# Shift filter of k in 32-row TensorE tiles, with compact diagonals, 1,024-wide gating, 512 KB exchanges and fourteen dummy matmul groups

## The chip, the cores and the metric

One core of one Trainium2 chip runs the whole kernel. The metric is the device time of one execution in microseconds (us). The kernel before takes 215.59 us in the median of its first three runs (215.18 to 217.14), and between 214.3 and 215.4 in the median of the later groups of runs. In the profile PE is TensorE (matmul), PEld its weight loads, DVE is VectorE, ACT is ScalarE, POOL is GpSimd and SP is SyncE, which issues the DMA transfers.

## The reference

Two blocks with residuals over x of 2,048 positions by 512 features, bf16. Cut to what matters:

```python
def _A_ref(q, k, v, shift_k, ssm_k, ssm_D):           # q is the layernorm of x
    k_pad = jnp.pad(k, ((0, 0), (ks - 1, 0), (0, 0)))  # ks = 4 taps
    for t in range(ks):                                # the shift filter of k
        k_shift = k_shift + k_pad[:, t:t + S, :] * shift_k[:, ks - 1 - t][None, None, :]
    kv = k_shift * v                                   # the gating
    y = irfft(rfft(kv, 2 * S) * rfft(ssm_k, 2 * S))[:S]   # a long convolution, feature by feature
    return q * (y + kv * ssm_D)
h  = x + _A_ref(layernorm(x), ...)
h2 = h + _B_ref(layernorm(h), w1, w2, w3, w4)          # two gelu MLPs, 512-512-512 and 512-1792-512
```

## The kernel before

The convolution is a Fourier transform in two steps on TensorE. Step 1 (`S1`) transforms within blocks; ScalarE or VectorE evacuates each result from PSUM (`E1`); an exchange by DMA (`X`) moves the parts to the partitions where step 2 (`S2`) needs them; its results are evacuated (`E2`), multiplied (`P`) and transformed back (`I2`, `EV`, an exchange `XI`, `I1`). `F0` is the convolution kernel, `A0` and `A1` are kv's first and second half. After it come the MLPs (`W`, `X2`, `M`, `O`). The time order of all tasks on all engines is fixed by a list in the source, `ORDER`, and semaphores keep it; so each engine runs its own tasks strictly in turn.

The shift filter (`K`) runs on TensorE as multiplication with diagonal matrices that hold the taps: k^T is the stationary operand (128 features by 128 positions) and four 128x128 diagonals of taps are the moving one. VectorE then multiplies with v (`KV`).

```python
    def fill(e, sl):                                       # a dummy group: keeps TensorE busy in waits
        for i in range(6):
            nc.tensor.matmul(ps[:, sl[0], 0:P], lhsT=ident[:], rhs=ident[:], start=True, stop=True)
    ...
        for g in range(2):
            for kl in range(4):
                def f(e, s, g=g, kl=kl):                   # one exchange: 256 KB, two of four blocks
                    nc.sync.dma_start(z2[sig][g:P:2, kl, :, :], z1[sig][kl:P:4, 2 * g:2 * g + 2, :, :])
    ...
    def shift(g, c):                                       # 16 groups: g = half and its half, c = 128 features
        s, b4 = divmod(g, 2)
        def f(e, sl):
            o = ps[:, sl[0], :]                            # one PSUM bank, 512 columns
            for i, d in enumerate((0, 1, 2, 3, -1, -2, -3)):   # 7 matmuls
                j0, j1 = max(0, -d), min(3, 3 - d)
                ...
                nc.tensor.matmul(o[:, (d + j0) * P:(d + j1 + 1) * P], lhsT=kT[s][c][:, bb, x:x + P],
                                 rhs=diag[:, c, j0:j1 + 1, :].rearrange("p j x -> p (j x)"), start=(i == 0), stop=(i == 6))
        return f
    def gating(g, c): ...                                  # 16 multiplies of 512
```

In an `ORDER` word the letter is the engine. `M` is a special one: it merges two evacuations of 1,024 columns into one of 2,048 on ScalarE.

Of the kernel before, what the change touches and what calls it, by code (L numbers as in the profile page):

```python
# [9 lines left out]
P = 128  # L10
# [3 lines left out]
DC = D // P  # L14
# [17 lines left out]
031V 002S 021P7 022P 027P6 059P01 005S 061P23 060A 041V 003S 063P45 065P67 033V 037V 099P10 091P01 000S 042G 001S 032V 043V 049V 062A 066A 008S 036G  # L32
040V 046V 055P23 057P67 064A 105P5 007S 035G 039A 047V 056A 010S 058A 103P4 106V 006S 034G 038A 048A 050V 004S 067P23 068A 069P67 070A 097P5 009S 018S
100V 044V 092V 098V 051A 045A 104V 101P1 019S 102V 093P0 094V 346V 095P5 096V 119P23 120A 115P01 116V 015S 117P67 118A 012S 121P45 122A 107P23 011S
108V 109P01 111P67 112V 113P45 110A 017S 344V 348V 114A 183P30 184V 013S 072S 076S 082P0167 084A 187P5 029P4 071S 075S 079P2367 020S 350V 128S 185P4
347V 188V 083A 127S 123S 053G 081A 124S 080A 351V 186V 125S 131P0167 133V 132A 343G 134P2345 136A 028P1 026P7 129S 137P0145 135A 016S 138A 054G 143V0
144V1 145P67230 147V2 139A 130S 146V3 148P 153V0 152V1 156V2 077S 149A 191P11 150A 073S 085P4567 087A 030P0 074S 192V 155V3 154P01231 157P 025P7 086A
158M 159A 349V 345V 024P6 126S 140P4567 141A 078S 151S 162V0 088P0123 089A 014S 161V1 160S 164V2 142V 352G 353G 354G 163P45670 165V3 170V0 166P 189P1
090A 171V1 174V2 168A 173V3 193P0 190V 172P23671 175P 177V 197P1 198V 167A 169S 052A 176A 178S 203P45 204A 205P67 206A 355G0 194V 195P3 196V 199P01
201P45 202A 358G1 340S 207P23 237S 200V 211P67 212A 217S 213P01 179P54 359V 364G1 180P76 356V 214A 361G0 235S 023P1 365V 208A 238S 236S 209P23 360A  # L40
357A 181P54 210A 362V 370V1 371V 379G 380G 367V0 366A 247P01 248A 249P23 376G1 363V 239P67 250A 182P10 240A 381V 251P23 377V 339S 382V0 252A 241P67
242A 392G 393G 219S 385V1 368V 373G0 383P00 386P4 387A 243P23 245P67 369A 372V 405G 406G 244A 253P45 254A 384V 390P0 391A 394V 395V0 396P31 398V1 374V
375A 399P2 246A 216S 397V 388P1 389A 400V 215S 223P2345 403P0 225A 378V 418G 407V 408V0 222S 221S 409P70 404A 411V1 412P6 220S 218S 224V 260S 262S
256S 413V 410V 275V0 401P1 402A 257S 276V1 278V2 229P2345 230A 419G 420G 424V0 259S 231A 414P7 415A 416P6 421V1 417A 266P0123 268V 267V 422P50 425P4
426A 261S 435P7 423A 436V 437A 431P6 432V 269P2345 433A 429P1 271V 430A 279V3 427P7 428A 232P4501 234A 342S 270V 233A 455G 439P7 440V 441A 443P6 444V
445A 456G 457G 461G0 255S 263P0123 264V 451P7 452V 265V 458G1 459P60 226P4501 460A 462P6 447P7 484G 485G 486V 228A 463A 258S 487V0 277P01230 280P
488A1 227A 281V0 282V1 285V2 341S 284V3 464P60 465A 474P5 490S 475A 283P 448V 290V0 286P 288A 272P4567 449A 291V1 273V 287A 453A 640G 641G 472P3 294V2
473A 476P2 292P01451 293V3 295P 274V 489S 477A 491S1 492P30 493A 496P7 296V0 497A 502P6 503A 642G 644A0 297V1 299V2 298P 300V3 306V0 301P 303A 302A
498P7 305V1 500P6 501A 504P5 505A 499A 446V 494P4 289S 307P01230 308V2 309V3 311V0 304S 310P 646S 495A 509P7 312V1 313P 438V 315V2 643V0 645S 314V3
316P 317M 318A 506P6 321V0 510V0 320V1 323V2 511S 322P01231 513S 324V3 325P 326V0 470P7 471A 327V1 329V2 468P5 469A 466P4 512S 330V3 518V 328P 331P  # L50
519V 467A 478P7 481P5 514S 516V 517V 332M 333A 521V 515S 522V 319S 523V 647S1 520V 524V 525G 442V 507V0 526V 530V0 334S 335P64 531V 532A 527G1 336P32
337P10 648P40 528V 529A 649A 536G0 537V 533G1 551V 552G 650P6 652P2 534V 542A0 543V 539G1 538A 653A 535A 651A 548A0 553V 554V0 660P4 658P3 659A 654P0
655A 555P60 557V1 540V 558P2 559A 541V 564G 565G 656P1 544V 576G 566V 556A 568V0 570S 567V1 338P03 545A1 546V 549V 569S 657A 577G 578V 661A 579V0 581S
580V1 582S 560P6 561A 482V1 483S 547A 550A 588G 589G 562P2 590G 662P4 571S0 563A 600P6 604P5 605V 606A 591G0 665P3 583S1 601V 574P6 575A 572P5 573A
592G1 584P2 585A 602V 586P6 587A 668V 450V 593S 669G 670V 671A0 616P6 617V 672G1 594S 595S0 596P5 597A 598P6 599A 620P2 434V 479V1 624P5 618V 636P7
621V 623V 622A 696V 628P6 697G 637V 674S 673S 632P2 675S0 676P70 686P1 480S 682P0 698V 700A0 699V1 701S 625V 626A 612P5 633V 702S 629V 678P6 608P2
677A 703S1 680P7 609V 630A 454V 724V 725G 683A 679A 638A 688P6 689A 726G 727A0 663V1 687A 664S 681A 611V 728V1 730S 613V 634V 780G 729S 684P2 685A
603V 704P00 712P6 705A 710P4 666V1 713A 614A 708P5 706P7 707A 714P3 610V 752V 711A 508S 731S0 709A 690P2 691V0 692S 716P7 732P60 744P2 781G 782G 753G
667S 693P5 754G 755A0 619V 756V1 758S 742P4 717A 745A 639V 733A 715A 734P7 735A 721P6 740P7 718P3 757S 722V0 738P6 736P2 759S1 784G1 760P10 772P0 607V
694V1 766P5 695S 737A 739A 770P6 635V 783G0 785S 723S 741A 743A 746P7 773A 762P4 786S 787S0 788P20 800P0 789A 801A 719V1 627V 767A 792P3 720S 793A  # L60
790P2 791A 798P5 799A 796P0 797A 794P3 795A 771A 747V0 748S 764P5 768P0 769A 805P7 806V0 749P0 807S 765A 761A 763A 631V 750V1 615V 751S 774P7 775V0
776S 802P6 803V1 804S 777P7 778V0 779S
# [40 lines left out]
def body(ctx, tc, fx, kt, q, v, sd, w1, w2, w3, w4, out):  # L103
# [69 lines left out]
    diag = r_dg[:].rearrange("p (c j x) -> p c j x", c=DC, j=4)  # L173
# [7 lines left out]
    hbt = ct("hbt", 2, D)  # L181
    junk = {"A": ct("junka", D, dt=mybir.dt.uint8), "V": ct("junkv", D, dt=mybir.dt.uint8)}
# [57 lines left out]
    make_identity(nc, ident[:])  # L240
    ui, us = ti[0][:, 0:512], ti[1]
# [10 lines left out]
    for o, terms in enumerate((((4, 16), (2, 8), (0, 4), (1, 2), (5, 1)), ((6, 64), (7, 1)), ((3, -1024), (7, 3072)), ((3, 3072),),  # L252
                               ((5, 4), (6, 8), (0, 128), (1, 256), (2, 512), (3, 1024), (4, 2048)), ((5, 64), (0, 16), (1, 32), (7, 1)),
                               ((3, -3072), (7, 3072)), ((4, 2), (2, 1)))):
        for b, w in terms:
            pool.memset(wf[:, o, b:b + 1], float(w))
# [50 lines left out]
    for i in range(8):  # L307
        add(("fill", i), {PEc: 0.36}, fill, ["wend"], take=[("ps", 1)], drop=[(("fill", i), 0)])
# [5 lines left out]
    def dg(c):  # L314
        def f(e, sl):
            for j in range(4):
                sc = sskf[:, 4 * c + j:4 * c + j + 1]
                if e == GP:
                    pool.tensor_scalar(out=diag[:, c, j, :], in0=ident[:], scalar1=sc, scalar2=0.0, op0=MUL, op1=ADD)
                elif e == A:  # L320
                    act.activation(diag[:, c, j, :], ident[:], ACT.Copy, scale=sc)
                else:
                    vec.tensor_scalar(out=diag[:, c, j, :], in0=ident[:], scalar1=sc, scalar2=None, op0=MUL)  # L323
        return f
    for c in range(DC):
        add(("dg", c), {V: 0.8, A: 1.19, GP: 1.45}, dg(c), [("skf", c)], port="VG")
# [82 lines left out]
    def forward1(sig, src, sdeps, zdeps, xdeps=(), sdrop=None):  # L409
# [7 lines left out]
        for g in range(2):  # L417
            for kl in range(4):
                def f(e, s, g=g, kl=kl):
                    nc.sync.dma_start(z2[sig][g:P:2, kl, :, :], z1[sig][kl:P:4, 2 * g:2 * g + 2, :, :])  # L420
                add(("X", sig, g, kl), {SP: 0.62}, f, [("E1", sig, b, hp) for b in (2 * g, 2 * g + 1) for hp in range(2)] + list(xdeps), size=256)
# [10 lines left out]
    def forward2(sig):  # L432
        for kl in range(4):
            n = ("S2", sig, kl)
            add(n, {PEc: 0.46}, step2(sig, kl), [("X", sig, g, kl) for g in range(2)] + ["ft"], take=[("ps", -2)], mode=2)
# [11 lines left out]
    def shift(g, c):  # L447
        s, b4 = divmod(g, 2)

        def f(e, sl):  # L450
            o = ps[:, sl[0], :]
            for i, d in enumerate((0, 1, 2, 3, -1, -2, -3)):
                j0, j1 = max(0, -d), min(3, 3 - d)
                bb, x = 4 * b4 + d, 1
                if bb < 0:
                    bb, x = bb + NB, 0
                nc.tensor.matmul(o[:, (d + j0) * P:(d + j1 + 1) * P], lhsT=kT[s][c][:, bb, x:x + P],  # L457
                                 rhs=diag[:, c, j0:j1 + 1, :].rearrange("p j x -> p (j x)"), start=(i == 0), stop=(i == 6))
        return f
# [396 lines left out]
```

## Time and profile before

| stage (before), us | what runs | what limits it |
|---|---|---|
| 4.5 to 17.4 | loads, transform of the convolution kernel, first half's filter | ScalarE, VectorE, DMA |
| 17.4 to 47.7 | first half's transforms and products, second half's filter | ScalarE |
| 47.7 to 80.6 | inverse, second half's transform, first MLP | ScalarE and TensorE |
| 80.6 to 208.6 | rest of the second half, MLPs | TensorE alone |

The lines of the profile behind this table are in the prediction below. One more from the page, its part on the DMA queues (packets, MB, share of 16 engines):

```profile
q8 instruction: 19, 0.31, 0.6%
```

### The profile page before, as it was taken

How to read it: one execution, taken by the hardware profiler on the slowest of the kernel's cores; microseconds unless marked ns; L12 is line 12 of the kernel's file. 1: busy time of each engine (PE TensorE's matmuls, PEld its weight loads, DVE VectorE, ACT ScalarE, POOL GpSimd, SP SyncE). 2: the span in 40 equal slices, each digit the busy share in tenths (PEclk: the TensorE clock that was granted, in tenths of full speed). 3: DMA queues.
4: the chain of work that ended last, by engine and by line, in shares of the span. 5: the costliest groups of instructions: out<-in, count | busy, mean ns of one | idle time of the engine just before them, and what ended most of it. 6: DMA issues, size and time to landing. Idle time of an engine off the chain costs nothing.

```text
span 212.1 us, 5986 instructions
## 1 busy us (share of the span) xinstructions
PE 198.5 (94%) x2418; PEld 120.5 (57%) x2436; DVE 142.6 (67%) x324; ACT 131.4 (62%) x211; POOL 60.1 (28%) x159
## 2 busy tenths in 40 slices
PE   7899888899899988999999999989999999999993
PEld 5454434543375536874554874756786657686441
DVE  7899999877999989968797883468484043100521
ACT  4998899989999777791360992445484303067000
POOL 7431004915980442300005776301161200000000
PEclk9999999999999999999999999999999999999999
DMA  6999896279939972613493027355235505100101
GB/s 183 301 400 354 311 332 216 104 219 331 400 149 324 354 312 56 151 47 104 144 233 99 3 53 152 79 109 107 49 102 82 118 0 125 51 25 3 47 28 49
DMA packets 31773, 33.44 MB, mean 158 GB/s; under 512 B 22529, under 2 KB 24578, under 8 KB 31490
## 3 DMA queue, kind: packets, MB, share of 16 engines
q1 hardware_dynamic: 31746, 33.06, 50.8%
q8 instruction: 19, 0.31, 0.6%
q14 instruction: 8, 0.07, 0.1%
HBM read 13.13 MB, written 4.72 MB: 84 GB/s over the span
## 4 chain that ended last, share of the span: by engine, by line
PE 64%; DMA 4%; DVE 4%; POOL 2%; ACT 2%; issue 2%; SPq 1%; DVEq 0%; POOLq 0%
PE ps L781 23%; PE ps L793 23%; PE ps L730 5%; PE ps L501 5%; DMA r_y<-r_x 4%; PE ps L701 3%; PE ps L520 2%; POOL z_t L619 1%; DVE r_v L622 1%; PE ps L457 1%; ACT r_h L705 1%; SPq L420 1%; PE ps L404 1%; ACT r_x L266 1%; DVE hbt L656 1%
## 5 line engine op out<-in xcount | busy, mean ns | idle before, releaser
L781 PE MATMUL ps<-r_dg,r_k 128*128 128x256 bf16 x448 | 51.4, 273 | 0.6 <-ACT r_vs L266 0.5
L781 PEld LDWEIGHTS <-r_k 128*128 128x128 bf16 x448 | 43.4, 98 | 8.9 <-issue 2.1
L795 DVE TENSOR_TENSOR r_kv<-ps,r_a 128x512 bf16<-128x512 f32 x5 | 3.5, 692 | 29.7 <-PE ps L793 29.7
L785 ACT ACTIVATE r_kv<-ps 128x512 bf16<-128x512 f32 x21 | 11.8, 601 | 17.2 <-PE ps L781 17.2
L793 PE MATMUL ps<-w4s,r_kv 128*128 128x512 bf16 x81 | 18.8, 379 | 0.2
L266 ACT CAST r_x<-ps 128x1024 bf16<-128x1024 f32 x16 | 15.4, 1026 | 2.3 <-PE ps L404 2.3
L730 PE MATMUL ps<-r_v,r_h 128*128 128x512 bf16 x59 | 15.0, 379 | 1.0 <-ACT r_h L705 0.7
L501 PE MATMUL ps<-r_p,ttab 32*32 32x512 bf16 x768 | 15.1, 379 | 0.8 <-DVE r_p L489 0.4
L457 PE MATMUL ps<-r_dg,r_k 128*128 128x256 bf16 (+3 forms) x109 | 15.3, 286 | 0.5 <-DVE r_dg L323 0.2
L701 PE MATMUL ps<-hnT,r_v 128*128 128x256 bf16 x128 | 15.6, 273 | 0.1
L793 PE MATMUL ps<-w4s,r_f 128*128 128x512 bf16 x62 | 15.0, 379 | 0.1
L266 ACT CAST r_f<-ps 128x1024 bf16<-128x1024 f32 x15 | 14.7, 1033 | 0.5 <-PE ps L428 0.4
L701 PEld LDWEIGHTS <-r_v 128*128 128x128 bf16 x128 | 12.1, 98 | 4.1 <-issue 2.3
L457 PEld LDWEIGHTS <-r_k 128*128 128x128 bf16 x112 | 9.2, 98 | 8.4 <-issue 4.2
L785 ACT ACTIVATE r_f<-ps 128x512 bf16<-128x512 f32 x16 | 9.0, 603 | 7.3 <-PE ps L781 7.2
L793 PEld LDWEIGHTS <-r_kv 128*128 128x128 bf16 x84 | 8.1, 98 | 9.5 <-issue 0.2
L705 ACT ACTIVATE r_h<-ps 128x512 bf16<-128x512 f32 x16 | 9.7, 641 | 4.9 <-PE ps L701 4.9
L501 PEld LDWEIGHTS <-ttab 32*32 32x32 bf16 x768 | 8.3, 88 | 7.0 <-issue 4.9
L607 ACT ACTIVATE junka<-r_q 128x512 uint8<-128x512 bf16 x12 | 7.6, 633 | 7.3 <-DVE r_q L733 7.0
L489 DVE TENSOR_TENSOR r_p<-r_a,r_y 128x1024 bf16<-128x1024 bf16 x16 | 10.1, 685 | 2.9 <-PE ps L501 2.8
L266 ACT CAST r_y<-ps 128x1024 bf16<-128x1024 f32 x12 | 11.4, 1021 | 1.2 <-PE ps L404 1.2
L404 PEld LDWEIGHTS <-f 128*32 128x32 bf16 x256 | 6.1, 95 | 10.3 <-issue 5.7
(179 smaller groups left out, 362.6 us busy)
## 6 DMA issues: line engine op xcount, KB each, us to landing
r_x<-r_vs SPq DMA_DIRECT2D x8, 512.0 KB, 3.3
r_k<-in_kt_dram SPq DMA_DIRECT2D x8, 259.0 KB, 6.2
r_v<-in_v_dram SPq DMA_DIRECT2D x4, 512.0 KB, 7.3
r_q<-in_q_dram SPq DMA_DIRECT2D x8, 256.0 KB, 5.4
r_f<-r_x SPq DMA_DIRECT2D x8, 256.0 KB, 5.2
r_a<-r_y SPq DMA_DIRECT2D x8, 256.0 KB, 3.7
r_f<-r_y SPq DMA_DIRECT2D x8, 256.0 KB, 4.1
r_y<-r_x SPq DMA_DIRECT2D x8, 256.0 KB, 2.4
```

Source lines behind the costliest of these rows:

```text
L266: (act.copy if e in "AM" else on[e].tensor_copy)(o, i)
L404: nc.tensor.matmul(ps[32 * j:32 * j + 32, sl[hh], :], lhsT=f1t[:, 4 * t + 2 * hp + hh, :], rhs=src(2 * b + b0), start=True, stop=True)
L457: nc.tensor.matmul(o[:, (d + j0) * P:(d + j1 + 1) * P], lhsT=kT[s][c][:, bb, x:x + P], rhs=diag[:, c, j0:j1 + 1, :].rearrange("p j x -> p ...
L489: on[e].tensor_tensor(out=prs[:, sl[0], :, :], in0=sp[a][:, kl, t, :, :], in1=gv, op=MUL)
L501: nc.tensor.matmul(ps[c:c + 32, bk[h], :], lhsT=ttab[32 * h:32 * h + 32, 2 * kl + t, 2 if x else xx, 32 * b0:32 * b0 + 32], rhs=prs[32 * h ...
L607: act.activation(junk[A][:], x, ACT.Square, scale=D ** -0.5, accum_out=sq[:, i, 1:2])
L701: nc.tensor.matmul(ps[:, sl[0], j * 256:(j + 1) * 256], lhsT=w1s[:, k, m * P:(m + 1) * P], rhs=hnT[:, k_, k, :], start=(k == 0), stop=(k = ...
L705: act.activation(h1T[:, 2 * h:2 * h + 2, 2 * p:2 * p + 2, 1 + P * s:1 + P * s + P], ps[:, got(("W", s, p, h))[0], :].rearrange("p (j b x) ...
L730: nc.tensor.matmul(ps[:, sl[0], :], lhsT=h1T[:, m, bb, x:x + P], rhs=w2s[:, m, :], start=(m == 0), stop=(m == DC - 1))
L781: nc.tensor.matmul(ps[:, sl[0], j * 256:(j + 1) * 256], lhsT=w3s[:, k, fc * P:(fc + 1) * P], rhs=lnT[:, k_, k, :], start=(k == 0), stop=(k ...
L785: act.activation(gb(gi, 2 * fp, 2), ps[:, got(("M", s, p, fp))[0], :].rearrange("p (j x) -> p j x", j=2), ACT.Gelu_apprx_tanh)
L793: nc.tensor.matmul(ps[:, sl[0], :], lhsT=gb(gi, fc)[:, 0, (b % 2) * P:(b % 2 + 1) * P], rhs=w4s[:, fc, :], start=(fc == 0), stop=(fc == FC ...
```

## The change

The intent is to use only the part of the diagonals that is not zero. Of a 128x128 diagonal, 127 of 128 entries are zero; a diagonal of 32 rows needs only 32 columns. So a matmul of 32 features streams a quarter of the columns, and two of them are to run side by side in row tiles of the array. The price is four times as many matmuls: 448 in place of 112, each with its weight load; a "pair" here and in the prediction is one matmul with its weight load. Around it, the gating is done 1,024 wide (8 multiplies for 16), the diagonals are built by four small multiplies in place of sixteen, exchanges move 512 KB (16 for 32), six more dummy groups are put into TensorE's waits, and `ORDER` is made anew. Core of the diff, cuts marked:

```diff
-    diag = r_dg[:].rearrange("p (c j x) -> p c j x", c=DC, j=4)
+    diag = view(r_dg, 0, DC * P, "p (c j x) -> p c j x", c=DC, j=4)     # 32 columns per tap
...
-    for i in range(8):
+    for i in range(14):
         add(("fill", i), {PEc: 0.36}, fill, ["wend"], take=[("ps", 1)], drop=[(("fill", i), 0)])
...
-        for g in range(2):
-            for kl in range(4):
-                def f(e, s, g=g, kl=kl):
-                    nc.sync.dma_start(z2[sig][g:P:2, kl, :, :], z1[sig][kl:P:4, 2 * g:2 * g + 2, :, :])
+        for kl in range(4):
+            def f(e, s, kl=kl):
+                nc.sync.dma_start(z2[sig][:, kl, :, :], z1[sig][kl:P:4, :, :, :])
...
-    def shift(g, c):
+    def shift(g, k):                          # 8 groups of 56 matmuls, two PSUM banks
...
+            for c in range(DC):
+                for i, d in enumerate((0, 1, 2, 3, -1, -2, -3)):
+                    ...
+                    for u in range(2):        # two row tiles in turn
+                        r = 32 * (2 * k + u)
+                        nc.tensor.matmul(ps[:, sl[u], :].rearrange("p (j x) -> p j x", j=4)[:, d + j0:d + j1 + 1, 32 * c:32 * c + 32],
+                                         lhsT=kT[s][c][r:r + 32, bb, x:x + P], rhs=diag[r:r + 32, c, j0:j1 + 1, :], start=(i == 0), stop=(i == 6))
...
-        for c in range(DC):
+        for k in range(2):                    # gating: 2 of 1,024 per g, not 4 of 512
...
 ORDER: all new; three evacuations are merged (M) in both kernels: EV.0.1 and two more of EV before, E2.A0.1, E2.F0.3 and one more of E2 after
```

## The prediction

> **What bounds the kernel now.** I read the busy shares first, then a table by stage (I set its borders where the work changes), then the timeline and order of each engine, then the waits. The shares alone mislead:

> ```profile
> PE 198.5 (94%) x2418; PEld 120.5 (57%) x2436; DVE 142.6 (67%) x324; ACT 131.4 (62%) x211; POOL 60.1 (28%) x159
> ```

> TensorE at 94% suggests that each microsecond of matmul removed is a microsecond won. The table by stage corrects this. Its columns are the window, its length, then busy us (instructions) of PE, PEld, DVE, ACT, POOL, the clock, the DMA share and GB/s:

> ```profile
> 4.50:17.40 12.90, 11.35 (x126) 6.17 (x123) 11.82 (x34) 11.87 (x19) 5.13 (x14) 1.00 0.98 350
> 17.40:26.50 9.10, 8.20 (x138) 3.92 (x139) 8.77 (x12) 8.47 (x9) 0.00 (x0) 1.00 0.84 322
> 26.50:47.70 21.20, 18.77 (x456) 9.27 (x457) 18.89 (x27) 20.53 (x22) 7.98 (x14) 1.00 0.66 218
> 47.70:68.60 20.90, 19.98 (x247) 10.70 (x245) 18.66 (x50) 20.85 (x34) 12.37 (x27) 1.00 0.82 299
> 68.60:80.60 12.00, 10.72 (x170) 5.33 (x171) 10.85 (x24) 8.92 (x17) 4.83 (x12) 1.00 0.80 306
> 80.60:208.60 128.00, 125.91 (x1270) 82.06 (x1280) 69.67 (x161) 58.88 (x109) 26.08 (x49) 1.00 0.35 83
> ```

> Two kernels in one. From 80.6 us TensorE alone is the bound (125.9 of 128.0). Before it, ScalarE has nearly no gap (20.5 of 21.2, then 20.85 of 20.9), VectorE is close behind, and until 17.4 us the DMA engines are full as well (0.98). All of the shift filter (L457) lies in this front: its first matmul is at 6.8 us, its last at 45.0. So what counts is how much sooner the front ends, not how much TensorE is relieved. Where the filter sits:

> ```profile
> 6.78 1.92 PE L457 MATMUL ps<-r_dg,r_k 128*128 128x512 bf16 x13
> ...
> 12.17 1.05 PE L404 MATMUL ps<-r_h,f 128*32 128x512 bf16 x16 [0.39 <-DMA r_h<-in_fx_dram]
> 13.15 3.66 PE L457 MATMUL ps<-r_dg,r_k 128*128 128x512 bf16 x28
> 16.73 4.18 PE L404 MATMUL ps<-r_kv,f 128*32 128x512 bf16 x64
> ...
> 23.26 0.50 PE L306 MATMUL ps<-ident 128*128 128x128 bf16 x6
> ...
> 47.72 1.90 PE L520 MATMUL ps<-r_x,f 64*128 64x512 bf16 x16
> ```

> Part of it fills time in which TensorE waits for data anyway, as the dummies of L306 do (8 groups of six). The first row with weight for the end is 47.72: the inverse transform of the first half starts there, and all later work hangs on it.

> [...]the six dummies, each with its own weight load, take 0.50 us, (500 - 219)/5 = 56 ns a step. [...]a load is recorded with 87 ns for 32x32, 89 for 64x32, 96 for 128x32, and 98 for 128x128. So a 32x128 load should not be costly. [...]16 matmuls of 64 rows in two row tiles take 1.90 us, 0.38 + 7 x 0.216, as if only eight ran in turn. [...]The gating of 512 shows 0.682 us[...].

> **The change part by part.**
> TensorE, shift filter. Before: 16 groups of 7 matmuls over 2,048 columns[...]; the group view shows 15.3 with the drains. After: 8 groups of 56, which alternate between two row tiles. In one row tile a feature block has N = 128, then twice 96, 64, 32[...]; the other tile runs beside it. 8 x 1.0 plus five drains of 0.15 (an estimate, the recorded latency less a step) = 8.7 us. Saved: 6.6 us. Six further dummy groups add 6 x 0.34 = 2.0; the order puts two of the fourteen behind the last real matmul, where they cost nothing, and most others in waits.

> VectorE. Gating: 16 x 0.60 (start to start) = 9.6 becomes 8 x 1.14 = 9.1[...]. Diagonals: eight 128x128 multiplies, 0.72 + 0.76, become four over 128 elements, estimated at 4 x 0.22 = 0.9. The angle table of L379 (0.90) goes to GpSimd. Against that one evacuation of 1.13 more (by the order, eight instead of seven ahead of the first half's h) and a q normalisation of 0.35. Net about -0.9.

> ScalarE, ahead of the last evacuation of the second half's first transform (L266, ended 52.2). It loses eight diagonal multiplies (2 x 1.28 = 2.5 us at 8.8 and 11.8 us) and one evacuation of 0.93. The gelu table load (1.28 + 0.20 at 41.3 us, in the gapless stretch) moves to just after the first evacuations of the filter's second transform, where ScalarE waits for the exchange. Work in this stretch by the order: 41 x 0.93 + 2.5 + 2.0 of sines + 1.5 = 44.1 us before, 40 x 0.93 + 2.0 + 1.5 = 40.7 after.

> DMA. Same bytes in exchanges, 16 of 512 KB for 32 of 256 KB. The issue table gives the landing times:

> ```profile
> r_x<-r_vs SPq DMA_DIRECT2D x8, 512.0 KB, 3.3
> ...
> r_f<-r_x SPq DMA_DIRECT2D x8, 256.0 KB, 5.2
> r_a<-r_y SPq DMA_DIRECT2D x8, 256.0 KB, 3.7
> r_f<-r_y SPq DMA_DIRECT2D x8, 256.0 KB, 4.1
> r_y<-r_x SPq DMA_DIRECT2D x8, 256.0 KB, 2.4
> ```

> A 512 KB move lands in 3.3 us in the median already, and half as many issues of 0.6 us save the queue's time. But none may now start before all four blocks are evacuated; before, half started two to three us sooner. The first group of the filter also waits for all four chunks of k and all diagonals.

> The front by hand: the last chunk of k, the eighth load instead of the ninth, lands near 10 us; three groups to 13.3, the fourth to about 15; the first transform of kv is evacuated at about 20.3 instead of 22.1; its exchange, whole only then, lets the next transform start near 25 instead of 25.86, and ScalarE begins the 17 evacuations that end this stage at about 26.2, almost as before (26.5). Without the table load 17 x 0.93 = 15.8 brings it to 42.0; before, it was 43.7. With the 4 us from that evacuation to L520 (43.7 to 47.7) the inverse starts near 46.0 instead of 47.7: -1.7. After it ScalarE, freed of the evacuation and the table load, is about 2.3 ahead, and TensorE has one 0.5 us transform less to do behind that point.

> So the front ends 2 to 3 us sooner. The back has the same matmuls, 125.6 us by counting groups at their measured rates, and one dummy group of 0.34 in the middle stage counts against it. Sum: 1.7 + 0.6 to 1.2 - 0.3 = about 2.5 us. 215.6 - 2.5 = 213.1, and a little for gaps that TensorE may lose: 212.8.

> **The rivals.**
> (a) TensorE's whole saving arrives: 215.6 - 6.6 + 0.7 of dummies = 209.7, 2.7% faster. For it: 94%, 19.98 of 20.9 in the fourth stage, and a chain of waits that is 64% TensorE. Against it: the filter is over before that stage, and ScalarE has only about 0.7 us of gap between 26.5 and 47.7.
> (b) The coarse exchanges give it back: four of them, each 1 to 3 us later, would hit ScalarE where it already waited for the first (0.44 us) and DMA r_y<-r_x, 9.5 us in the chain of waits at 65.9, where loads of w3 and w4 stand in the queue. That makes 214 to 218. Against it: the 3.3 us landing, and other TensorE work that lies ready.
> (c) The 448 small pairs don't pack: [...]a group 2.8 us, and the fourth group would end near 20 us: 217 to 221. Against it: 64 pairs of 32x32 in 16 tiles run in 1.10 us, 17 ns a pair.

> **Range and chances.** The hand count gives 212.8; half of (a) and a mild (b) span 208.8 to 217.0. Over 2% faster needs 211.3, which takes half of the difference between the count and (a): 0.30. Over 2% slower needs (c) or a strong (b): 0.05. The rest, 0.65.

> **What would show it.** Right: a filter group near 1.0 us and its line at 8 to 9 us busy; gating at 1.22 us; ScalarE still above 95% between the first exchange and the fourth stage; the first L520 (L519 there) near 46; then as many us to the end as before. Wrong: the inverse at 43 or less (rival a, the front was bound by TensorE); ScalarE gaps of over a microsecond that end with a 512 KB exchange (b); a group of 1.5 us or more (c); or TensorE's idle time after 47 us changing by more than a microsecond.

## The result

The changed kernel gives correct results and takes **225.65 us** in the median of 4 runs (223.43 to 226.19), beside 215.38 (214.36 to 217.14) of the kernel before: ratio 1.0448, 95% interval 1.0349 to 1.0547. It is 4.5% slower; the prediction was 212.8, with 217.0 as the upper end. A ratio here and below is the mean time of one kernel's fast runs over that of the other's fast runs of the same rounds, so it is not quite the ratio of the medians quoted beside it.

Shares of the changed kernel, and the row of the granted TensorE clock in 40 slices of 5.6 us (9 is full speed, 5 about half):

```profile
PE 203.1 (91%) x2808; PEld 124.2 (56%) x2808; DVE 144.6 (65%) x310; ACT 125.7 (56%) x198; POOL 59.6 (27%) x172
...
PEclk9985796799999999999999999999999999999999
...
q8 instruction: 22, 0.36, 0.7%
```

TensorE, relieved of most of its filter columns, is busy *longer* than before (203.1 us for 198.5). The six more dummy groups are some 3 us of it; the clock row says why beyond that: in the third to fifth and in the seventh and eighth slices the clock is down, which it never was in the kernel before, whose row has a 9 in every slice. And there are three more packets of instructions, 22 for 19. Three windows, up to the inverse, up to the last MLP and behind (same columns as in the prediction):

```profile
26.70:58.10 31.40, 24.84 (x714) 13.33 (x710) 24.51 (x35) 26.55 (x28) 5.66 (x11) 0.89 0.60 209
58.10:88.20 30.10, 27.95 (x349) 14.92 (x346) 26.93 (x64) 27.83 (x50) 18.86 (x40) 1.00 0.88 319
88.20:220.00 131.80, 129.69 (x1352) 83.00 (x1351) 75.95 (x169) 56.25 (x105) 24.19 (x58) 1.00 0.31 80
```

ScalarE is busy for 26.55 of 31.40 us up to the inverse; before, it had nearly no gap there. So it is no longer ScalarE that sets the front. TensorE's timeline shows what does (start, busy us, line, what, count, and in brackets the idle time before it and what ended it):

```profile
10.65 2.32 PE L452 MATMUL ps<-r_dg,r_k 32*128 32x128 bf16 x129
16.43 1.33 PE L452 MATMUL ps<-r_dg,r_k 32*128 32x96 bf16 x39 [3.47 <-issue]
...
18.52 1.07 PE L398 MATMUL ps<-r_kv,f 128*32 128x512 bf16 x8
19.52 1.89 PE L452 MATMUL ps<-r_dg,r_k 32*128 32x128 bf16 x56
21.35 4.45 PE L398 MATMUL ps<-r_kv,f 128*32 128x512 bf16 x48
...
34.19 0.63 PE L421 MATMUL ps<-r_a,ftab 64*32 64x512 bf16 x16 [1.44 <-DMA r_a<-r_y]
36.80 1.44 PE L308 MATMUL ps<-ident 128*128 128x128 bf16 x12 [1.99 <-ACT r_a L276]
38.17 1.05 PE L421 MATMUL ps<-r_a,ftab 64*32 64x512 bf16 x16
...
58.11 2.12 PE L519 MATMUL ps<-r_x,f 64*128 64x512 bf16 x18
```

Four things are to be seen. First, 129 of the three groups' 168 filter matmuls run in 2.32 us, 18 ns a pair, just as fast as hoped; then TensorE stands still for 3.47 us in the *middle of a group*, and the releaser is "issue": nothing that the profile shows was waited for. Second, work after it takes nearly twice its time: 56 pairs 1.89 us, and 16 transform matmuls (L421, at 38.17) 1.05 us where the kernel before needs 0.63. Third, at 34.19 a wait of 1.44 us ends with an exchange (r_a<-r_y, now 512 KB). Fourth, at 36.8 there is a wait of 1.99 us for L276, the merged 2,048-wide evacuation. The engine behind TensorE waits in turn; ScalarE:

```profile
18.79 1.01 ACT L268 CAST r_x<-ps 128x1024 bf16<-128x1024 f32 x1 [4.93 <-PE ps L398]
...
34.89 1.86 ACT L276 CAST r_a<-ps 128x2048 bf16<-128x2048 f32 x1 [0.97 <-PE ps L421]
39.30 1.93 ACT L268 CAST r_a<-ps 128x1024 bf16<-128x1024 f32 x2 [2.55 <-PE ps L421]
```

The filter's and the gating's groups of the whole run (busy us, mean ns, idle before):

```profile
L452 PE MATMUL ps<-r_dg,r_k 32*128 32x96 bf16 (+3 forms) x448 | 10.5, 204 | 3.6 <-issue 3.5
...
L463 DVE TENSOR_TENSOR r_kv<-ps,r_v 128x1024 bf16<-128x1024 f32 x8 | 9.6, 1217 | 6.5 <-PE ps L452 5.3
```

Where the time went, as start times of the same milestones in the timelines of the profiled runs (us):

| milestone | before | after | difference |
|---|---|---|---|
| end of the last step-1 matmul of kv's first half | 20.91 | 26.67 | +5.8 |
| third step-2 matmul group of kv (`S2.A0.2`) | 28.36 | 38.17 | +9.8 |
| inverse of the first half (`I1.0`) | 47.72 | 58.11 | +10.4 |
| last matmul of the last MLP ends | 208.54 | 220.01 | +11.5 |

Nearly all of it arises before 38 us. The rest of this document is about these two steps: 5.8 us at the filter, 4.0 us between the transforms. The second step has two halves: the second step-2 group follows the first after 2.65 us (0.57 before), with the wait for the exchange in it, and the third follows the second after 3.98 us (1.93 before), with the wait for the merged evacuation.

### The profile page after: what moved, and what is told of

Read it like the earlier page. It is cut to its first block, busy times and chain, and to the rows that moved or that the text cites.

```text
span 223.6 us, 6700 instructions
## 1 busy us (share of the span) xinstructions
PE 203.1 (91%) x2808; PEld 124.2 (56%) x2808; DVE 144.6 (65%) x310; ACT 125.7 (56%) x198; POOL 59.6 (27%) x172
## 5 line engine op out<-in xcount | busy, mean ns | idle before, releaser
L780 PEld LDWEIGHTS <-r_k 128*128 128x128 bf16 x448 | 43.1, 98 | 10.5 <-issue 2.9
L268 ACT CAST r_x<-ps 128x1024 bf16<-128x1024 f32 x15 | 14.7, 1021 | 7.8 <-PE ps L398 7.8
L268 ACT CAST r_vs<-ps 128x1024 bf16<-128x1024 f32 x14 | 13.8, 1014 | 5.7 <-issue 3.8
L794 DVE TENSOR_TENSOR ob<-ps,r_a 128x512 bf16<-128x512 f32 x5 | 3.5, 691 | 20.6 <-PE ps L792 16.6
L784 ACT ACTIVATE r_f<-ps 128x512 bf16<-128x512 f32 x16 | 9.1, 595 | 13.3 <-PE ps L780 13.3
L500 PE MATMUL ps<-r_p,ttab 32*32 32x512 bf16 x768 | 15.6, 399 | 0.8 <-ACT r_f L276 0.7
L784 ACT ACTIVATE r_y<-ps 128x512 bf16<-128x512 f32 x12 | 7.0, 602 | 14.1 <-PE ps L780 14.1
L463 DVE TENSOR_TENSOR r_kv<-ps,r_v 128x1024 bf16<-128x1024 f32 x8 | 9.6, 1217 | 6.5 <-PE ps L452 5.3
L452 PE MATMUL ps<-r_dg,r_k 32*128 32x96 bf16 (+3 forms) x448 | 10.5, 204 | 3.6 <-issue 3.5
L452 PEld LDWEIGHTS <-r_k 32*128 32x128 bf16 x448 | 9.7, 101 | 6.5 <-issue 6.1
L488 DVE TENSOR_TENSOR r_p<-r_a,r_f 128x1024 bf16<-128x1024 bf16 x16 | 10.1, 684 | 4.1 <-ACT r_a L268 4.1
## 6 DMA issues: line engine op xcount, KB each, us to landing
r_x<-r_vs SPq DMA_DIRECT2D x8, 512.0 KB, 3.7
r_v<-in_v_dram SPq DMA_DIRECT2D x4, 512.0 KB, 7.8
r_q<-in_q_dram SPq DMA_DIRECT2D x8, 256.0 KB, 5.5
r_f<-r_x SPq DMA_DIRECT2D x4, 512.0 KB, 5.7
r_a<-r_y SPq DMA_DIRECT2D x4, 512.0 KB, 6.0
r_f<-r_y SPq DMA_DIRECT2D x4, 512.0 KB, 4.9
r_y<-r_x SPq DMA_DIRECT2D x4, 512.0 KB, 9.8
```

What stands on the lines that cost most here:

```text
L268: (act.copy if e in "AM" else on[e].tensor_copy)(o, i)
L452: nc.tensor.matmul(ps[:, sl[u], :].rearrange("p (j x) -> p j x", j=4)[:, d + j0:d + j1 + 1, 32 * c:32 * c + 32], lhsT=kT[s][c][r:r + 32, b ...
L463: vec.tensor_tensor(out=lay(kvs[:, got(("K", g, 0), "kv")[0]]), in0=pair(got(("K", g, k))).rearrange("p r (b x) -> p r b x", b=4), in1=lay ...
L488: on[e].tensor_tensor(out=prs[:, sl[0], :, :], in0=sp[a][:, kl, t, :, :], in1=gv, op=MUL)
L500: nc.tensor.matmul(ps[c:c + 32, bk[h], :], lhsT=ttab[32 * h:32 * h + 32, 2 * kl + t, 2 if x else xx, 32 * b0:32 * b0 + 32], rhs=prs[32 * h ...
L780: nc.tensor.matmul(ps[:, sl[0], j * 256:(j + 1) * 256], lhsT=w3s[:, k, fc * P:(fc + 1) * P], rhs=lnT[:, k_, k, :], start=(k == 0), stop=(k ...
```

## The experiments

**Theory.** The stop is a missing instruction block. The filter's pairs are issued at some 120 instructions per microsecond, and the next block, brought by a DMA that stands behind full queues, comes too late. TensorE's pause, and later waits, then cost half of its clock for a while. **Rivals:** R1, the new order and the coarse exchanges are what costs; R2, the small row tiles themselves stop TensorE; R3, the idle time is harmless and only the count of matmuls matters.

All runs below gave a correct result by the comparison. Times are medians; the kernels of one group were timed beside the same runs of the kernel before, whose median is given.

### First group (before: 214.34)

**e1_full_rows**: the new order, exchanges and gating, but the filter as before, with full diagonals (all sixteen built on VectorE).

```diff
+                    nc.tensor.matmul(ps[:, sl[u], :][:, (d + j0) * P:(d + j1 + 1) * P], lhsT=kT[s][c][:, bb, x:x + P],
+                                     rhs=diag[:, c, j0:j1 + 1, :].rearrange("p j x -> p (j x)"), start=(i == 0), stop=(i == 6))
```

> The changed kernel with the old 128-row matmuls and full diagonals, in the new order, with the 1024-wide gating, the 512 KB exchanges and the fourteen dummies kept: 672 TensorE instructions fewer. Theory F (TensorE ran out of instructions at 12.97 us, because the 16 KB refill came late, and the gap then halved its clock): no gap of over 1 us inside the filter, the clock at 1.00 from 5 us on, the inverse transform at 45 to 48 us instead of 58.1, 211 to 216 us in all. Theory C (the exchanges, which now start whole): the inverse still at 55 or later, 221 us or more. Theory O (the new order as such): the same as C.

Measured: 221.05 us (218.53 to 221.86), ratio 1.0263 [1.0157, 1.0369]. The profiled run was the slowest of the four, so its times are used with care.

```profile
10.88 5.40 PE L453 MATMUL ps<-r_dg,r_k 128*128 128x512 bf16 x42
...
32.82 0.83 PE L308 MATMUL ps<-ident 128*128 128x128 bf16 x12 [2.07 <-ACT r_a L276]
```

Three groups of the old matmuls take 5.40 us without a break, and still the loss against the kernel before is 2.6% and not 4.5%, some 4 us less, though the two intervals overlap slightly. So the four-fold filter seems to cost time rather than save it. But this run speaks for R1: its inverse starts at 55.40 us and it takes 221.05, which is what the theories of the exchanges and of the order had said, and not 45 to 48 and 211 to 216. Its clock is down once (34.4 to 37.8 us), and the 2.07 us wait for the merged evacuation is here as well.

**e2_busy**: sixteen 512-wide dummies ahead of the second filter group, so that TensorE has work while the block comes.

```diff
+            if (g, k) == (1, 0):
+                for _ in range(16):
+                    nc.tensor.matmul(ps[:, 2, :], lhsT=ident[:], rhs=fxs[0][:, 0, :], start=True, stop=True)
```

> The changed kernel with sixteen 512-column dummy matmuls (3.5 us) after the first filter group, so that TensorE is busy, not idle, while the second refill of instructions is under way; the filter ends no sooner. F: the stall inside the filter shrinks from 3.47 us to under 1, TensorE's clock is not halved at 14.55 us, and the time falls by 3 to 7 us, which is then the share of the clock. If the 32-row matmuls as such let the clock drop: half clock near 14.5 us as before, time within 1% of the changed kernel. C: within 1%.

Measured: 224.97 us (220.59 to 225.08). Three of four runs lie over 1.5% above the fastest and count as slow, so there is no ratio; the profiled run is one of the slow ones. The 3 to 7 us that were expected did not come.

```profile
12.48 3.61 PE L456 MATMUL ps<-r_h,ident 128*128 128x512 bf16 x16 [0.84 <-ACT r_x L268]
16.02 2.06 PE L452 MATMUL ps<-r_dg,r_k 32*128 32x128 bf16 x112
```

The stop is gone: the dummies fill its time and 112 pairs then run in 2.06 us. The filter ends hardly later (18.0 for 17.7), the clock stays up until 28.2 us, and the last step-1 matmul of kv ends at 24.02 for 26.67, 2.65 us sooner. That is the clock's share of the first loss. The clock fell three times later (28.2, 35.0 and 96.4 us, 3.4 us each), and most of the gain was lost again. For this stretch R3 falls: with more matmuls it ends sooner.

**e3_quiet**: five loads (two of k, two of q, one of v) moved behind the first exchange, with the tasks that read them.

```
ORDER: Lk.1.2 Lk.1.0 Lq.0.0 Lq.0.3 Lv.1.0 moved behind X.F0.0.1;  Q.0.0 Q.0.7 Q.0.1 moved ahead of Q.0.6
```

> The changed kernel with five loads that nothing needs before 24 us (1.5 MB of q, k and v for later) issued after the first exchange instead of before it, so that the DMA queues are quieter from 9 to 15 us. Not an instruction of TensorE changes. F: [...]the stall of 3.47 us falls to under 2, the time by 2 to 8 us. C and O: stall or not, the time stays within 1% (or grows, as the loads come later).

Measured: 226.02 us (224.67 to 227.04), ratio 1.053 [1.0452, 1.0608].

```profile
12.47 3.25 PE L454 MATMUL ps<-r_dg,r_k 32*128 32x128 bf16 x168
...
28.96 2.99 PE L454 MATMUL ps<-r_dg,r_k 32*128 32x128 bf16 x98 [4.39 <-DMA r_k<-in_kt_dram]
```

The same 448 small matmuls in the same tiles, and all 168 of the first three groups run through with no stop. R2 falls: the tiles as such don't stop TensorE. Two things differ: the block landed 2.15 us sooner, and the filter began 1.82 us later (the clock was down from 8.76 to 12.17 us, ahead of it). The last step-1 matmul ends at 21.58 for 26.67. But the later k came too late, and 4.39 us were lost there: as an improvement it failed, and the 2 to 8 us less that were expected did not come.

**e4_coarse**: the kernel before with exchanges of 512 KB alone (each put at the place of the later of its two halves; a table of weights is swapped to match the new order of partitions).

```diff
-                    nc.sync.dma_start(z2[sig][g:P:2, kl, :, :], z1[sig][kl:P:4, 2 * g:2 * g + 2, :, :])
+                    if g == LATE[sig, kl]:
+                        nc.sync.dma_start(z2[sig][:, kl, :, :], z1[sig][kl:P:4, :, :, :])
```

> The kernel before with the 512 KB exchanges alone: each pair of 256 KB moves made one, at the place of the later one in the order. F: within 2% of before (213 to 219 us), full clock. C: 219 us or more.

Measured: 215.53 us (215.22 to 216.18), ratio 1.0049 [0.9986, 1.0111]. Coarse exchanges in the old order cost about 1 us, if anything: by themselves they are not the 10 us. Its trace has one stop of 0.98 us with the releaser "issue" (at 35.40 us), so even this 1 us need not be the exchanges'.

### Second group (before: 215.22)

**e5_wide**: as few instructions as the row tiles allow: one 512-wide matmul per feature block and tile, 64 in place of 448, in the new order. It computes only part of the filter. Its output is wrong, which doesn't matter for the time. The comparison passes it all the same, so that passing proves nothing about this kernel.

```diff
+                    nc.tensor.matmul(ps[:, sl[u], :], lhsT=kT[s][c][r:r + 32, 4 * b4, 1:1 + P],
+                                     rhs=diag[r:r + 32].rearrange("p c j x -> p (c j x)"), start=(c == 0), stop=(c == DC - 1))
```

> The changed kernel with each filter group made of eight 32-row matmuls of 512 columns instead of 56 of 32 to 128 ([...]768 instructions fewer; the result is wrong on purpose). F (refill late, then half clock): no stall in the filter, no half clock at 14.55 us, the last transform of kv ends near 20 to 21.5 us instead of 26.1. As the first run with full rows showed that the new order has a loss of its own (its inverse at 55.4 us without any stall), I expect the inverse near 50 to 53 us and 214 to 218 us in all. If the order as such holds it back: 219 or more.

Measured: 216.83 us (215.38 to 217.59), ratio 1.0065 [1.0011, 1.012]. With 768 instructions fewer, the loss falls from 4.5% to 0.7%. A half-clock stretch from 28.2 to 38.5 was left.

**e6_rows64**: a correct filter with half the instructions: tiles of 64 rows, 28 matmuls a group (224 in all), both row tiles in use.

```diff
-                        r = 32 * (2 * k + u)
+                        r = 64 * u
...
+                        nc.tensor.matmul(ps[:, sl[u], :].rearrange("p (j x) -> p j x", j=4)[:, d + j0:d + j1 + 1, 64 * ci:64 * ci + 64],
+                                         lhsT=kT[s][c][r:r + 64, bb, x:x + P], rhs=diag[r:r + 64, c, j0:j1 + 1, :], start=(i == 0), stop=(i == 6))
```

> The changed kernel with 64-row tiles: the same two row tiles side by side, diagonals 64 wide, 28 matmuls a group instead of 56, correct. [...]half the instructions. F: the stall of 3.47 us falls to under 2 and moves behind the third group; half clock shorter or gone; 4 to 8 us less than the changed kernel's 225. Rival (the stall is not one of instructions): as the changed kernel within 1%.

Measured: 217.57 us (216.91 to 217.86), ratio 1.0103 [1.0061, 1.0146].

```profile
10.71 3.08 PE L452 MATMUL ps<-r_dg,r_k 64*128 64x256 bf16 x84
...
29.59 1.44 PE L307 MATMUL ps<-ident 128*128 128x128 bf16 x12 [2.07 <-ACT r_a L275]
```

Three groups need 3.08 us, about the array time that the 32-row groups would need (2.32 us for 129 of 168 makes 3.0), without a stop. Step 1 of kv ends at 19.89, a microsecond *sooner* than in the kernel before. This is the change as it was meant. The loss falls from 4.5% to 1.0% with half the instructions. What is left sits at 29.59: the wait for the merged evacuation, and a half clock from 29.2 to 32.7.

**e7_pad and e8_ctl**: the reverse test in the kernel before. e7 puts 21 tiny matmuls (8 columns) ahead of each of the 16 filter groups, which makes as many instructions as the change; e8 puts two 512-wide ones there, hardly any instructions.

```diff
+            for n in range(21):                                                                              # e7_pad
+                nc.tensor.matmul(o[:, 0:8], lhsT=ident[0:32, :], rhs=ident[0:32, 0:8], start=True, stop=True)
+            for n in range(2):                                                                               # e8_ctl
+                nc.tensor.matmul(o[:, 0:512], lhsT=ident[:], rhs=fxs[0][:, 2, :], start=True, stop=True)
```

> The kernel before, with 21 tiny 32-row matmuls of 8 columns put ahead of each of the 16 filter groups (672 instructions more, as many as the change added to the filter; the result stays right). F: gaps that end with nothing but issue appear among them, 1 us or more, the clock may fall; 4 us or more slower than its twin with two long matmuls. Rival: within 2% of the twin.

> Twin of the padded kernel: the kernel before with two 512-column dummies (0.43 us) ahead of each filter group, about the array time of the 21 tiny ones, but 64 instructions instead of 672. Both theories: 216 to 221 us, full clock, no gap of instructions.

Measured: e7 223.62 us (223.57 to 224.46), ratio 1.0402 [1.0351, 1.0452]; e8 219.97 (218.89 to 220.51), ratio 1.0213 [1.0163, 1.0263]. This missed: e7's timeline has no stop and no drop of the clock. Its bursts are

```profile
7.38 0.68 PE L453 MATMUL ps<-ident 32*128 32x8 bf16 x21
```

and a filter group of seven takes over a microsecond between two of them. The same number of instructions, spread out, is supplied in time; and e7's 3.7 us over its twin are mostly the bursts' own length (0.61 us from a burst's start to its filter group's, against 0.43 in e8; 16 of these differences make 2.9 us). So the theory had to be made narrower: not the number of instructions counts, but how many are issued in one run before a block can come. The closer test, the same row tiles in the order of the kernel before, was not run.

### Third group (before: 215.04)

**e9_unmerged**: e6_rows64 with the merged evacuation cut into two again, one letter in `ORDER`.

```diff
-... 125M 126A ...        (E2.A0.1, both parts in one ScalarE instruction of 2,048)
+... 125A 126A ...        (two of 1,024)
```

> The changed kernel with 64-row filter tiles (as e6_rows64) and, besides, the merged 2,048-wide evacuation of the second transform of kv cut into two of 1,024, as the kernel before has them. Theory: what e6_rows64 still loses between the second transform's start and the first inverse column (6.5 us there, 3.2 before) comes from that one evacuation, which holds four banks: TensorE waits 2.1 us for it and its clock falls after it. Then the third transform of kv starts near 28.5, no clock drop at 28 to 33 us, and the time is 214.5 to 216 (e6_rows64: 217.6). Rival: the loss is the later filter groups and exchanges in the order; then the first inverse column stays at 31.5 or later and the time is at 217 or above.

Measured: **215.36 us** (214.52 to 217.18), ratio 1.0022 [0.9973, 1.0072]: the same as the kernel before. The clock is full to the end of the work.

```profile
PE 196.9 (92%) x2569; PEld 120.9 (57%) x2584; DVE 144.8 (68%) x310; ACT 125.7 (59%) x199; POOL 58.0 (27%) x170
...
27.07 0.62 PE L422 MATMUL ps<-r_a,ftab 64*32 64x512 bf16 x16 [1.17 <-DMA r_a<-r_y]
...
28.40 0.63 PE L422 MATMUL ps<-r_a,ftab 64*32 64x512 bf16 x16
```

`S2.A0.2` starts at 28.40 (30.95 in e6_rows64), as expected. What e6_rows64 still lost was this one evacuation and the clock drop that began in its wait. The new order and the coarse exchanges are all still in, so of R1 there remains the merge and the gain that did not come.

**e10_quiet2**: the changed kernel with three loads moved behind the first exchange, those of k left early: e3_quiet without its flaw.

```
ORDER: Lq.0.0 Lq.0.3 Lv.1.0 moved behind X.F0.0.1;  Q.0.0 Q.0.7 Q.0.1 moved ahead of Q.0.6
```

> The changed kernel with only three loads (two of q, one of v of the second half; 1.3 MB) moved behind the first exchange; the loads of k stay where they are, unlike in e3_quiet. Theory: the stop of TensorE in the third filter group is an instruction block that came late through full DMA queues; with 1.3 MB less in them it comes early enough: the gap without visible cause shrinks from 3.5 us to under 1.0, the last transform of kv before its exchange ends by 23 us instead of 26.7, and the time falls by 2 to 5 us to 220.5 to 223.5. Rival: the stop comes from the instructions themselves[...]; then it stays at 3 us and more, and the time above 224.

Measured: 225.24 us (223.45 to 226.52), ratio 1.0461 [1.0394, 1.0528]. By its numbers a miss: the stop shrank only to 2.05 us, and the time not at all.

```profile
9.97 2.06 PE L454 MATMUL ps<-r_dg,r_k 32*128 32x128 bf16 x112
12.28 0.50 PE L454 MATMUL ps<-r_dg,r_k 32*128 32x128 bf16 x17 [0.25 <-ACT r_x L270]
14.83 1.33 PE L454 MATMUL ps<-r_dg,r_k 32*128 32x96 bf16 x39 [2.05 <-issue]
```

Yet these lines are the best evidence for the theory's first half. TensorE stopped after 129 of 168 matmuls again, though it got there at another time, behind another wait. And set against the trace's records of the instruction queue, the end of the stop follows the block. The times of the first block that arrives in the trace, and of TensorE's traced instructions number 449 and 450 (matmuls, weight loads, and the few drain and semaphore instructions that the trace has, two of them at the start), in us:

| kernel | first block under way | 449th issued | 450th issued | 450th after the block's end |
|---|---|---|---|---|
| after | 14.03 to 15.03 | 12.77 | 16.43 | 1.40 |
| e10_quiet2 | 12.46 to 13.40 | 12.58 | 14.83 | 1.43 |
| e12_trim (below) | 14.39 to 15.36 | 16.26 | 16.95 | 1.60 |
| e6_rows64 | 13.65 to 14.68 | 16.09 | 16.15 | 1.47 |
| e11_both (below) | 13.48 to 14.47 | 15.67 | 15.90 | 1.43 |
| e9_unmerged | 13.09 to 14.04 | 15.60 | 15.63 | 1.59 |
| e3_quiet | 11.92 to 12.88 | 14.86 | 14.86 | 1.98 |
| e2_busy | 13.44 to 14.46 | 16.99 | 16.99 | 2.53 |
| before | 13.73 to 14.81 | 21.83 | 21.83 | 7.02 |

In no kernel is the 450th issued sooner than 1.40 us after the block has landed; in the five that the table leaves out it comes 4.1 to 10.3 us after. Where TensorE gets there earlier, it stops exactly there, whatever that instruction is: a filter matmul in two kernels, a step-1 transform in e12_trim. Where it gets there later, nothing happens. How many blocks TensorE had before the first one of the table is not shown; two of 256 (the spacing found below) would fit the 449 traced instructions if some 60 uncounted ones (registers, semaphores) went before, which is the author's estimate. Later blocks show the same limit, in two traces in the middle of a group of 64 matmuls of the transform back (`I2`):

```profile
35.41 0.39 PE L502 MATMUL ps<-r_p,ttab 32*32 32x512 bf16 x3 [0.63 <-issue]
36.69 0.39 PE L502 MATMUL ps<-r_p,ttab 32*32 32x512 bf16 x3 [0.75 <-issue]
```

The first is of e9_unmerged, the second of e12_trim. Both stops lie ahead of instruction 1,218 and end 1.34 and 1.31 us after the fourth block has landed; e12_trim stops at 450 after the first block too, so three blocks hold 768 instructions, 256 each. The stop in e4_coarse lies ahead of number 963 (450, twice 256 and one) and ends 1.49 us after the third block. So stops come where a block ends, in filter and transforms alike.

The changed kernel uses up the 256 instructions ahead of the stop in 2.1 us (10.65 to 12.77), the kernel before takes 11.1 us for the same ones.

Why the shorter stop won nothing: the clock fell from 13.7 to 24.0 us all the same, as long as in the changed kernel (14.5 to 24.8), and k again kept TensorE waiting 1.37 us at 27.7.

**e11_both**: e9_unmerged with the three loads moved.

> e9_unmerged with the three loads of e10_quiet2 moved as well. With half of the filter's matmuls there is no stop to remove, so by the theory of the instruction supply this gives nothing over e9_unmerged: within 1 us of it. Rival (the DMA share itself slows the front, whatever the instructions): 1 to 3 us faster than e9_unmerged.

Measured: 219.12 us (218.24 to 220.8), ratio 1.0189 [1.0145, 1.0232]. Neither side was right: it is slower than e9_unmerged. There was no stop to remove, and the k of the second half, which now stood behind q and v in the queue, kept TensorE waiting for 3.75 us. Moving loads in a full queue is not a small change.

### Fourth group (before: 215.05)

**e12_trim**: an attempt to beat both: e9_unmerged with the other merged evacuation of this stretch cut too and four dummy groups emptied.

```diff
-        add(("fill", i), {PEc: 0.36}, fill, ["wend"], ...)
+        add(("fill", i), {PEc: 0.36}, (lambda e, sl: None) if i in (3, 11, 6, 7) else fill, ["wend"], ...)
 ORDER: E2.F0.3.0 from M to A
```

> e9_unmerged, in the hope to beat both kernels: the merged evacuation ahead of the third exchange (E2.F0.3) is cut in two as well, and four of the fourteen dummy groups are emptied: two behind the last matmul, and the two in the stretch where TensorE is the bound. By the trace of e9_unmerged the two cost about 0.45 us each there, and the wait at the merged evacuation is 0.7 us. If these lie on the path, 1 to 1.5 us come off e9_unmerged: 213.9 to 214.5, 0.3 to 0.6% under the kernel before. If the waits move elsewhere, it is within 0.5 us of e9_unmerged; over 217 would mean that the dummies were what kept the clock up there.

Measured: 216.83 us (216.47 to 218.19), ratio 1.0089 [1.006, 1.0118]. The hope failed; by its ratio it is 0.7% slower than e9_unmerged, with intervals that overlap. In its trace the instruction limit shows twice, at 36.69 us (above) and here, for a transform:

```profile
16.26 0.39 PE L399 MATMUL ps<-r_kv,f 128*32 128x512 bf16 x1
16.95 3.63 PE L399 MATMUL ps<-r_kv,f 128*32 128x512 bf16 x55 [0.31 <-issue]
```

No experiment beat the kernel before; the best one equals it.

## Why the prediction was wrong

Taken by its own steps:

- **"What counts is how much sooner the front ends"**: right, and the sign of it wrong. The inverse started at 58.11, not at 46.0.
- **A filter group of 1.0 us, packing (rival c)**: right. The 1.0 us was the author's estimate; 112 pairs, two groups, ran in 2.06 us (e2_busy), 18 ns a pair, so c did not occur, and yet its range of 217 to 221 was exceeded: the loss came by a way that was in none of the rivals.
- **The step that failed: "three groups to 13.3, the fourth to about 15", and the first kv transform evacuated at 20.3.** The third group ended near 17.7 and the fourth at 21.4. The working counted the array's time and the waits on semaphores, and took it for granted that TensorE gets its instructions at any rate and keeps its clock. The runs showed two terms in their place. The first is a stop of 3.47 us for an instruction block (table above). The second is the clock: from 14.5 to 24.8 us TensorE was busy for 8.3 us at half speed, which at full speed would be 4.2, so at most some 4.1 us are the clock's; e2_busy, where the clock stayed up, gave 2.65. Together 6.1 to 7.6; the last step-1 matmul ended 7.3 us later than in e9_unmerged, which has neither up to there.
- **"17 evacuations from 26.2 gapless to 42.0"**: failed too, in two places. The second 512 KB exchange makes TensorE wait 1.44 us (to 34.19), and the order's merged evacuation 1.99 us for four banks (34.81 to 36.80). The clock is down from 35.0 to 41.9. In the 3.41 us ahead of this drop (31.6 to 35.0) TensorE was idle for 1.86, of which the exchange has 1.44 and the merged evacuation's wait only 0.22, so in the changed kernel itself the drop can't be put down to the merge; in e6_rows64, where 1.72 us of that wait lie ahead of the drop, it can. I had read this merge in the order and did not ask which matmul waits for its banks. Taking it apart in the 64-row version returned 217.57 to 215.36, about 2.2 us. It was not tried alone in the 32-row version.
- **Even without both, the predicted gain of 2.5 us did not come** (its own terms, 1.7 + 0.6 to 1.2 - 0.3, make 2.0 to 2.6). In e9_unmerged step 1 of kv ends 1.5 us sooner than before, but step 2 of kv starts only 0.6 us sooner (25.27 for 25.86), and its second group waits 1.17 us for a 512 KB exchange that takes 6.1 us in the median, where I had counted 3.3, read off another move. That is rival b, small. Its third group starts as before (28.40 for 28.36), and its inverse 0.9 us later (48.60 for 47.72); the stop of 0.63 us for a block lies in this stretch, and the rest was not taken apart. The exchanges' landing times in the changed kernel:

```profile
r_a<-r_y SPq DMA_DIRECT2D x4, 512.0 KB, 6.0
...
r_y<-r_x SPq DMA_DIRECT2D x4, 512.0 KB, 9.8
```

- **A 32x128 weight load that is not costly**: right. It is recorded with 93 ns in the median and 101 in the mean (after), for 98 of a 128x128 load (before).
- **The gating (1.22 us, estimate) and VectorE**: right, 1.217. **The back "as many us to the end as before"**: from the start of the inverse to the end 161.9 us for 160.8, close.
- **Rival a, TensorE's whole saving (6.6 us by estimate)**: no. e9_unmerged has it (its filter is busy for 8.33 us, for 15.32 before), and the time doesn't move; the front was not TensorE's, as argued.

What stays open is when exactly the clock falls. Each drop in the traces but the kernel's last lasts 3.4, 6.8 or 10.2 us (3.41 at 8.76 in e3_quiet; 6.83 at 35.0 and 10.24 at 14.5 in the changed kernel). TensorE was not idle ahead of them: in the 3.41 us that end within 0.05 us of a drop TensorE was busy for 1.88 us (after, 14.5), 2.24 (e10_quiet2, 13.7), 1.48 (e6_rows64, 29.2), and even

```profile
24.80:28.21 3.41, 2.77 (x128) 2.25 (x128) 3.05 (x5) 2.48 (x4) 0.00 (x0) 0.99 1.00 373
```

2.77 in e2_busy ahead of its drop at 28.2, most of it 32-row pairs: 43 to 81% of these 3.41 us. Yet e6_rows64 was busy for 1.77 in the 3.41 us to 8.76, without such pairs, and kept its clock. And the clock of the changed kernel stayed down (0.50) through a window in which TensorE had no gap (17.91 to 21.33, busy for 3.42 of 3.42 us). Whether pairs that fill only part of the array count for less was not shown; no run isolates it. Nor is it settled what sets the moment at which a block is fetched: it came 1.6 and 2.1 us sooner when loads were taken out of the early queues (e10_quiet2, e3_quiet), but in e7_pad, where none was, it came 2.4 us sooner than in the kernel before.

## What to carry to other kernels

When a matmul is cut into more and smaller ones, count the instructions in a run as well as the array's time: here 256 had to last longer than the 2.1 us that 32-row pairs took, and twice as tall tiles had about the same array time (3.08 us for three groups; 2.32 for 129 of 168 makes 3.0) with half the instructions. After any stop of TensorE look at the clock row before anything else, since here pauses of 3.47 us (after) and 2.05 us (e10_quiet2) went with half the clock over some 10 us (14.5 to 24.8 and 13.7 to 24.0). And ask of each saving whether its engine sets that stage's end, and of each merged evacuation which matmul is waiting for its banks.
